# Sparse attention with a SoLU layer on one core: queries copied so that a block's columns lie together, the last tile in two banks, a new order

## The chip, the cores and the metric

The kernel runs on one core of a Trainium2 chip. The metric is the device time of one execution in microseconds; the time before is the median of three runs, 487.01 us (484.95 to 489.06). Smaller is better.

## What is computed

Attention over 8 batches, 8 heads, 576 positions and a head size of 64, in which four heads see the last 32 positions (local) and four see the positions with the same remainder modulo 32 (strided); then, for the 4608 tokens, a layer with two matrices, a softmax gate and a normalisation. Cut to what matters:

```python
scores = np.matmul(q, k.transpose(0, 1, 3, 2)) / np.sqrt(D)
mask_local = (rel >= 0) & (rel < 32)
mask_strided = (rel >= 0) & (pos[None, :] % 32 == pos[:, None] % 32)
attn = softmax(np.where(masks, scores, -1e9))     # heads 0-3 local, 4-7 strided
x = (attn @ v).transpose(0, 2, 1, 3).reshape(B * S, H * D)
...
h = x @ w_in                                      # 512 -> 1024
solu = h * softmax(h)
ln = (solu - mean(solu)) / sqrt(var(solu) + 1e-6) * g_ln
out = ln @ w_out                                  # 1024 -> 512
```

## The kernel before

All work is cut into steps, each a function that issues the instructions of one engine, with the tiles that it reads and writes. `Plan.add` (L128) records them in the order in which the program is written; a table of step numbers, `ORDER` (L61), found by a search, gives the order in which they are issued. Each engine works through its own steps in that order, and semaphores keep the dependencies.

Attention goes by units: each batch has two strided ones (6 and 5 blocks; a block is 3 remainders times 18 positions, 54 queries against 54 keys) and two local ones (5 and 4 blocks of 64 queries against 96 keys; in batch 0 they are 3 and 6). A unit (`unit`, L419) writes the mask into PSUM (L454, ACT; in batch 0 by PE, L463), adds the scores in float32 on PE (`qk`, L469), subtracts the row maximum, takes the exponential (L498), sums, scales on POOL (L507), splits the result into two float16 halves (L527, L529), transposes them by DMA (L534; batch 0 turns them on PE instead) and multiplies by the values (`pv`, L561). In batch 0 the units use L481 to subtract the maximum by a matmul, and the values stay in float32. Head pairs are placed so that four matmuls of 64 by 64 use the array side by side.

The queries lie in memory by position within the block, `q_raw` (L174), so one block's columns of a strided unit are 22 numbers apart and those of a local unit 18:

```python
q_raw[half][hs, q0 : q0 + (w - 1) * nqb + 1 : nqb]
```

The layer goes by 36 tiles of 128 tokens (`ff`). `g1` (L625 to L627) multiplies a tile by `w_in` in two halves of h, 512 columns each, 12 matmuls each (float16 high and low parts); DVE takes the maximum (L631), ACT the exponential (L635), DVE the product (L637), ACT the normalisation (L641, L642), POOL its small factors (L651 to L675), ACT and DVE the two float16 parts (L682, L683), a DMA transposes them (L686), and `g2` (L695 to L697) multiplies by `w_out`; ACT scales and stores a tile (L703, L704). Three banks of PSUM hold halves of h, one holds the out product.

Both matrices come as 64 bit numbers and are turned to float32 by `decode` (ACT L734, POOL L739, DVE L740), four blocks each; `prep_w` (L743) then forms `whi` (ACT, L761) and `wlo` (DVE, L762), and `prep_o` (L766) sums squares of `w_out` on PE (L777) and forms `ohi` (L786) and `olo` (L787). `v_scale` (L371) takes the size of a batch's values (L377), `v_split` (L396) their two float16 parts (L402, L403). `warm` (L246) issues matmuls whose results nobody reads.

The last tile's product is in one bank. ACT scales and stores its left half (L710, L711), DVE its right half (L714), which SP stores (L715).

Of the kernel before, what the change touches and what calls it, by code (L numbers as in the profile page):

```python
# [890 lines left out]
```

## Time and profile before

| | us |
|---|---|
| median of three runs | 487.01 |
| the three runs | 484.95, 489.06, 487.01 |
| the profiled execution | 488.86 |
| its span, from the first to the last instruction | 487.1 |

The rows that the prediction uses stand in a section below. In a row of the timeline the columns are start, duration, engine, line, operation, output and inputs, shapes and count, and in brackets the idle time of the engine before it with what ended it. PE is the engine of the matmuls, DVE, ACT and POOL the vector, scalar and general engines, SP the one that only issues DMAs; a q behind an engine's name is its queue of issues. One row can stand for several instructions of a kind (xcount), and then its duration is that of all of them.

### The profile page before, as it was taken

How to read it: one execution, taken by the hardware profiler on the slowest of the kernel's cores; microseconds unless marked ns; L12 is line 12 of the kernel's file. 1: busy time of each engine (PE TensorE's matmuls, PEld its weight loads, DVE VectorE, ACT ScalarE, POOL GpSimd, SP SyncE). 2: the span in 40 equal slices, each digit the busy share in tenths (PEclk: the TensorE clock that was granted, in tenths of full speed). 3: DMA queues.
4: the chain of work that ended last, by engine and by line, in shares of the span. 5: the costliest groups of instructions: out<-in, count | busy, mean ns of one | idle time of the engine just before them, and what ended most of it. 6: DMA issues, size and time to landing. Idle time of an engine off the chain costs nothing.

```text
span 487.1 us, 15063 instructions
## 1 busy us (share of the span) xinstructions
PE 470.0 (96%) x6436; PEld 244.0 (50%) x6436; DVE 326.5 (67%) x698; ACT 336.3 (69%) x555; POOL 168.5 (35%) x328
## 2 busy tenths in 40 slices
PE   8867989999999999999999999999999999999996
PEld 3645655555555555455454555545545544444442
DVE  0889799898788776777758666776656474444430
ACT  2498699798878878867675885855776565565450
POOL 5465425452623432242152314331234242232220
PEclk9995998999999999999999999999999999999999
DMA  8998689678979996657996992678573786405332
GB/s 331 419 372 321 182 189 261 141 163 228 183 186 201 209 222 125 175 78 166 268 163 138 250 220 72 109 155 157 128 132 62 137 148 115 87 23 129 74 84 81
DMA packets 131763, 83.87 MB, mean 172 GB/s; under 512 B 117424, under 2 KB 118288, under 8 KB 131184
## 3 DMA queue, kind: packets, MB, share of 16 engines
q1 hardware_dynamic: 126512, 73.60, 65.5%
q10 hardware_dynamic: 5184, 9.31, 5.6%
q8 instruction: 50, 0.82, 0.7%
q14 instruction: 17, 0.14, 0.1%
HBM read 39.90 MB, written 9.44 MB: 101 GB/s over the span
## 4 chain that ended last, share of the span: by engine, by line
PE 87%; DVE 5%; DMA 5%; issue 1%; SPq 0%; ACT 0%; ACTq 0%
PE o_ps L695 12%; PE h_ps L625 12%; PE h_ps L626 12%; PE o_ps L697 12%; PE h_ps L627 12%; PE o_ps L696 12%; PE s_ps L469 6%; PE x_ps L561 5%; DMA vrs<-vstr 3%; DMA q<-qstr 2%; DVE w L762 1%; DVE obuf L740 1%; DVE m L476 0%; DVE m L499 0%; DVE st L631 0%
## 5 line engine op out<-in xcount | busy, mean ns | idle before, releaser
L695 PE MATMUL o_ps<-ohi,cc 128*128 128x512 f16 x272 | 103.3, 380 | 0.0
L697 PE MATMUL o_ps<-ohi,cc 128*128 128x512 f16 x272 | 103.1, 379 | 0.0
L696 PE MATMUL o_ps<-obuf,cc 128*128 128x512 f16 x272 | 103.1, 379 | 0.0
L631 DVE TENSOR_REDUCE st<-h_ps 128x1 f32<-128x512 f32 x70 | 47.3, 684 | 42.6 <-PE h_ps L627 40.5
L507 POOL TENSOR_TENSOR t<-t,m 128x540 f32<-128x540 f32 (+5 forms) x32 | 42.7, 1339 | 87.9 <-DVE m L504 74.0
L683 DVE SCALAR_TENSOR_TENSOR cc<-raw,st,cc 128x1024 f16<-128x1024 f32 (+1 forms) x38 | 46.6, 1232 | 30.1 <-ACT cc L682 30.0
L635 ACT ACTIVATE raw<-h_ps,st,vsc 128x512 f32<-128x512 f32 x62 | 47.9, 775 | 23.5 <-DVE st L633 22.5
L626 PE MATMUL h_ps<-w,xl 128*128 128x512 f16 x140 | 54.0, 386 | 1.8 <-DVE obuf L740 1.8
L637 DVE SCALAR_TENSOR_TENSOR raw<-h_ps,raw 128x512 f32<-128x512 f32 x70 | 47.0, 682 | 12.2 <-ACT raw L635 11.4
L625 PE MATMUL h_ps<-w,xl 128*128 128x512 f16 x140 | 54.2, 387 | 0.3 <-DVE raw L637 0.3
L682 ACT ACTIVATE cc<-raw,st 128x1024 f16<-128x1024 f32 (+1 forms) x38 | 41.6, 1100 | 18.3 <-POOL st L672 17.3
L627 PE MATMUL h_ps<-w,xl 128*128 128x512 f16 x140 | 54.1, 386 | 0.0
L625 PE MATMUL h_ps<-w,xs 128*128 128x512 f16 x140 | 53.6, 383 | 0.0
L626 PE MATMUL h_ps<-w,xs 128*128 128x512 f16 x140 | 53.5, 382 | 0.0
L627 PE MATMUL h_ps<-w,xs 128*128 128x512 f16 x140 | 53.1, 379 | 0.0
L641 ACT ACTIVATE raw<-raw,st 128x1024 f32<-128x1024 f32 x36 | 41.2, 1144 | 16.7 <-DVE st L640 13.8
L697 PEld LDWEIGHTS <-cc 128*128 128x128 f16 x288 | 28.1, 98 | 34.0
L703 ACT ACTIVATE ob<-o_ps,st 128x512 f32<-128x512 f32 x34 | 23.2, 683 | 31.7 <-PE o_ps L697 25.9
L695 PEld LDWEIGHTS <-cc 128*128 128x128 f16 x288 | 28.1, 98 | 33.0
L696 PEld LDWEIGHTS <-cc 128*128 128x128 f16 x288 | 28.2, 98 | 32.1
L670 POOL TENSOR_SCALAR st<-st 128x1 f32<-128x1 f32 x32 | 8.8, 275 | 88.7 <-ACT raw L642 88.0
L642 ACT ACTIVATE raw<-raw 128x1024 f32<-128x1024 f32 x36 | 37.9, 1054 | 2.2 <-ACT ob L703 1.7
(187 smaller groups left out, 841.1 us busy)
## 6 DMA issues: line engine op xcount, KB each, us to landing
out<-ob ACTq DMA_DIRECT2D x35, 256.0 KB, 3.5
k<-kstr SPq DMA_DIRECT2D x8, 594.0 KB, 5.2
q<-qstr SPq DMA_DIRECT2D x8, 594.0 KB, 5.9
k<-kloc SPq DMA_DIRECT2D x8, 576.0 KB, 5.7
q<-qloc SPq DMA_DIRECT2D x8, 576.0 KB, 6.4
raw<-w_in SPq DMA_DIRECT2D x4, 1024.0 KB, 6.8
ve<-vl SPq DMA_DIRECT2D x7, 480.0 KB, 4.0
vrs<-vstr SPq DMA_DIRECT2D x4, 768.0 KB, 6.3
```

Source lines behind the costliest of these rows:

```text
L507: add("pool", nx * nk / 520 + 0.03, lambda: nc.gpsimd.tensor_tensor(t4, t4, sm2.unsqueeze(3).broadcast_to([P, 2, nb, nk]), op=ALU.mult), r ...
L625: nc.tensor.matmul(hv[i], xhi[cc], whi[:, cc, cols], start=(cc == 0), stop=False)
L626: nc.tensor.matmul(hv[i], xhi[cc], wlo[:, cc, cols], start=False, stop=False)
L627: nc.tensor.matmul(hv[i], xlo[cc], whi[:, cc, cols], start=False, stop=(cc == 3))
L631: add("dve", 0.69, lambda i=i: nc.vector.tensor_reduce((nm, nm2)[i], hv[i], axis=AX.X, op=ALU.max, negate=True), r=[HH[i]], w=[(ST, "nm", i)])
L635: add("act", 0.73, lambda i=i, q=q: nc.scalar.activation(e[:, parts2[i]], hv[i], AF.Exp, bias=nm, scale=hs, accum_out=q), r=[HH[i], (ST, " ...
L637: add("dve", 0.7, lambda i=i, x=x: nc.vector.scalar_tensor_tensor(u[:, parts2[i]], hv[i], 1.0, e[:, parts2[i]], op0=ALU.mult, op1=ALU.mult ...
L682: add("act", w / 1200 + 0.295, lambda cols=cols: nc.scalar.mul(c[:, 0, cols], u[:, cols], r), r=[(U, 0), (U, 1), (ST, "r")], w=CC[0][mine])
L683: add("dve", w / 980 + 0.23, lambda cols=cols: nc.vector.scalar_tensor_tensor(c[:, 1, cols], u[:, cols], r, c[:, 0, cols], op0=ALU.mult, o ...
L695: nc.tensor.matmul(o, ct[:, cc, :], ohi[:, cc, :], start=(cc == 0), stop=False)
L696: nc.tensor.matmul(o, ct[:, cc, :], olo[:, cc, :], start=False, stop=False)
L697: nc.tensor.matmul(o, ct[:, 8 + cc, :], ohi[:, cc, :], start=False, stop=(cc == 7))
```

## The change

Queries first. From batch 2 on the strided queries are copied in float32, and in batches 6 and 7 the local ones too, so that the columns of a block are contiguous; the copies are on ACT for the strided ones of odd batches, on POOL otherwise. They lie in memory that was free at that time (`qc` behind the second set of raw values, `ql` in the unused half of `obuf`). The last tile's out product is cut at column 384 into two banks, and DVE writes its part into another buffer. Twelve more warm matmuls (`LATE`) can stand before `prep_o`. The order is searched anew for all steps. `V_PE` is empty, so the branch that it guards isn't taken; two cost entries of the plan change, which set no instruction by themselves.

```diff
+END = 384
+LATE = 6
+BLOCKED = (2, 3, 4, 5, 6, 7)
+BLOCKED_LOC = (6, 7)
 ORDER = """
-0-1 27 2 30 24 22 50 3-10 51 56 52 31 28 23 35 11 32-34 25 43 20 12 26 13 57 38 14-15 102 44 37 103-104 58 86 53 21
+1 3-5 39 31 28 6-9 22 2 34-35 20 44 32 27 23 33 10 46 29 56 11 79 30 86 102 45 87 103 25 88 104-105 38 12 58 57 13 106
...
+    ql = obuf[:, :, 256:512].rearrange("p c (x i) -> p c x i", i=QL)
+    qc = [more[:, VW[0] + VW[1] + i : VW[0] + VW[1] + j] for i, j in ((0, 12 * QS), (12 * QS, 2 * SP))]
+    NB2 = SP // QS
...
+    def by_block(b):
+        for j, (_, b0, nb) in enumerate(LATER[0:2]):
+            w = 2 * nb * QS
+            dst = qc[j][:, 0:w].rearrange("p (c x i) -> p c x i", c=2, x=nb)
+            src = q_raw[1][:, 0 : 2 * SP].rearrange("p (i c x) -> p c x i", c=2, x=NB2)[:, :, b0 : b0 + nb]
+            r, wr = [("q", 1)], [("qc", j), *([("roomq",)] if b == BLOCKED[0] else [])]
+            if b % 2:
+                add("act", w / 1200 + 0.3, lambda dst=dst, src=src: nc.scalar.copy(dst, src), r=r, w=wr)
+            else:
+                add("pool", w / 480 + 0.1, lambda dst=dst, src=src: nc.gpsimd.tensor_copy(dst, src), r=r, w=wr)
+
+    def local_by_block(b):
+        src = q_raw[0][:, 0 : 2 * S].rearrange("p (i x) -> p x i", x=2 * NBL)
...
+            nc.gpsimd.tensor_copy(ql[:, 0:4], src[:, 0:16].rearrange("p (c x) i -> p c x i", x=4))
+            nc.gpsimd.tensor_copy(ql[:, 4, 0 : 2 * NBL - 16], src[:, 16 : 2 * NBL])
...
+                        if blocked and not half:
+                            x = pair * NBL + b0 + i
+                            q = ql[hs, x // 4, x % 4, a : a + w]
+                        elif blocked:
+                            q = qc[j][hs, (pair * nb + i) * QS : (pair * nb + i + 1) * QS]
...
-        add("pe", nb * (0.212, 0.2)[half] + ((0.27, 0.14) if by_pe else (0.008, 0.195))[half], qk,
+        add("pe", nb * 0.145 + 0.195 if blocked and half else nb * (0.212, 0.2)[half] + ((0.27, 0.14) if by_pe else (0.008, 0.195))[half], qk,
...
+            sides = [(o[:, 0:END], O, slice(0, END)), (s_ps[:, 0, END:DM], ("s", 0), slice(END, DM))]
...
-            add("dve", 0.42, lambda: nc.vector.tensor_scalar(ob[:, ends[1]], o[:, ends[1]], f, None, op0=ALU.mult), r=[O, (ST, "f"), OB], w=[(*OB, 1)])
+            ob2, OB2 = e_sb[(n + 1) % 2], [(("e", (n + 1) % 2), y) for y in range(2)]
+            add("dve", 0.3, lambda: nc.vector.tensor_scalar(ob2[:, rc], right, f, None, op0=ALU.mult), r=[RIGHT, (ST, "f")], w=OB2)
...
+            for i in range(LATE):
+                add("pe", 0.4, lambda: warm(2, [h_ps[1][:, 0:480]]), r=["ones"], w=[("h", 1)])
```

Three places in the order. The first is SP's queue at the start of the program, before, where `w_in` and `w_out` are the matrices, `kstr` and `qstr` the strided keys and queries, `vloc` the local values:

```order
L346 DMA raw_67<-w_in 128x2048 x2
L268 DMA mask_80<-masks 128x288
L346 DMA k_66<-kstr 128x1188
L346 DMA q_64<-qstr 128x1188
L796 DMA g_119<-g 128x8
```

and now:

```order
L355 DMA vl_70<-vloc 128x1280
L277 DMA mask_80<-masks 128x288
L355 DMA q_64<-qstr 128x1188
L355 DMA k_66<-kstr 128x1188
L355 DMA raw_67<-w_in 128x2048 x2
```

Two blocks of `w_in` went from ahead of the strided queries and keys to behind them, and the local values came to the front.

The second is ACT in the start-up, around the last quarter of `whi` (the row that writes `w_114`); `obuf` is where `w_out` is turned to float32, `s_ps<-mask` the mask of the next unit. Before:

```order
L761 ACTIVATE w_114<-cc_104,w_sc_116 128x1024
L454 COPY s_ps<-mask_80 128x2x270
L522 ACTIVATE pt_99<-o_ps,vsc_76 128x384
L582 CAST xl_100<-x_ps 128x2x64
L582 CAST xl_100<-x_ps 128x2x2x64
L498 ACTIVATE t_85<-t_85 128x648
L734 ACTIVATE obuf_115<-raw_67 128x1024 x2
L402 ACTIVATE vs_72<-vrs_69,vsc_77 128x1536
L522 ACTIVATE pt_99<-h_ps,vsc_76 128x384
L734 ACTIVATE obuf_115<-cc_104 128x1024
L498 ACTIVATE t_86<-t_86 128x540
L454 CAST s_ps<-mk_loc_81 128x2x320
```

and now:

```order
L793 ACTIVATE obuf_115<-raw_67 128x1024
L793 ACTIVATE obuf_115<-cc_104 128x1024
L550 ACTIVATE t_85<-t_85 128x648
L634 CAST xl_100<-x_ps 128x2x64
L574 ACTIVATE pt_99<-h_ps,vsc_76 128x384
L550 ACTIVATE t_86<-t_86 128x540
L634 CAST xl_100<-x_ps 128x2x2x64
L499 CAST s_ps<-mk_loc_81 128x2x320
L820 ACTIVATE w_114<-cc_104,w_sc_116 128x1024
L579 CAST p_94<-t_85 128x12x54
L446 ACTIVATE vl_70<-vrl_68,vsc_77 128x1280
L400 ACTIVATE vs_71,vm_74<-raw_67 128x1536
```

What stood behind the last quarter stands ahead of it now.

The third is where the copies stand. On ACT, ahead of batch 5's first strided unit (its mask is the row `s_ps<-mask_80 128x2x324`; `raw_67,st` are the exponentials of an h tile), it reads before:

```order
L635 ACTIVATE raw_67,st_108<-h_ps,st_108 128x512
L682 ACTIVATE cc_104<-raw_67,st_107 128x1024
L641 ACTIVATE raw_67<-raw_67,st_108 128x1024
L454 COPY s_ps<-mask_80 128x2x324
L635 ACTIVATE raw_67,st_109<-h_ps,st_109,vsc_79 128x512 x2
```

and now:

```order
L446 ACTIVATE vl_70<-raw_67,vsc_76 128x1280
L550 ACTIVATE t_88<-t_88 128x512
L421 COPY raw_67<-q_64 128x648
L421 COPY raw_67<-q_64 128x540
L579 CAST p_96<-t_87 128x2x320
L499 COPY s_ps<-mask_80 128x2x324
L687 ACTIVATE raw_67,st_109<-h_ps,st_109,vsc_79 128x512 x2
```

The two copies stand three places ahead of the exponentials. On POOL, batch 2's copies now stand here, among the multiplies and subtractions of batch 1 (before, the same rows without them):

```order
L559 TENSOR_TENSOR t_86<-t_86,m_89 128x540
L581 TENSOR_TENSOR p_94<-t_85,p_94 128x12x54
L423 COPY raw_67<-q_64 128x648
L581 TENSOR_TENSOR p_95<-t_86,p_95 128x2x5x54
L423 COPY raw_67<-q_64 128x540
L704 TENSOR_SCALAR st_107<-st_107 128x1
```

The small steps of the first tile's norm follow them.

## Rows read from the trace of the kernel before

**Rows 1.** The page: the span, then busy us, share and instructions by engine.

```profile
span 487.1 us, 15063 instructions
...
PE 470.0 (96%) x6436; PEld 244.0 (50%) x6436; DVE 326.5 (67%) x698; ACT 336.3 (69%) x555; POOL 168.5 (35%) x328
```

**Rows 2.** Stages: length, busy us (x instructions) by engine, clock, DMA share, GB/s.

```profile
core 0: us, PE busy (x) PEld busy (x) DVE busy (x) ACT busy (x) POOL busy (x), PEclk, DMA share, GB/s
72.00:76.00 4.00, 3.88 (x17) 1.61 (x18) 4.00 (x8) 3.97 (x8) 0.00 (x0) 0.57 0.84 117
200.00:220.00 20.00, 20.00 (x134) 9.49 (x132) 14.41 (x31) 13.41 (x22) 6.15 (x14) 1.00 0.65 127
460.00:480.00 20.00, 20.00 (x94) 9.05 (x93) 5.91 (x12) 8.29 (x14) 2.62 (x8) 1.00 0.38 93
```

**Rows 3.** PE in order of time: half of an h, later a strided scores unit.

```profile
144.17 0.38 PE L625 MATMUL h_ps<-w,xl 128*128 128x512 f16 x1
...
146.76 0.38 PE L625 MATMUL h_ps<-w,xl 128*128 128x512 f16 x1
...
150.39 1.46 PE L469 MATMUL s_ps<-k,q 64*54 64x54 f32 x48
151.79 0.39 PE L625 MATMUL h_ps<-w,xl 128*128 128x512 f16 x1
```

**Rows 4.** PE in order of time, in the first 46 us.

```profile
11.55 1.26 PE L469 MATMUL h_ps<-k,q 64*54 64x54 f32 x40 [1.14 <-DMA q<-qstr]
...
15.52 0.63 PE L753 MATMUL x_ps<-cc 128*128 128x128 bf16 x8 [0.27 <-DVE cc L740]
...
19.71 1.27 PE L469 MATMUL h_ps<-k,q 64*32 64x64 f32 x96
...
30.54 0.92 PE L561 MATMUL x_ps<-pt,vs 54*64 54x54 f32 x48 [0.76 <-ACT pt L522]
...
45.77 0.59 PE L626 MATMUL h_ps<-w,xl 128*128 128x512 f16 x1 [1.84 <-DVE obuf L740]
```

**Rows 5.** Groups of one line by form: busy us, mean ns of one.

```profile
L481 PE MATMUL h_ps<-m,minus 128*128 128x384 f32 x4 | 1.5, 485 | 0.0
...
L481 PE MATMUL s_ps<-m,minus 128*128 128x192 f32 x4 | 0.9, 338 | 0.0
```

**Rows 6.** Groups of ACT and of POOL: operations of a unit's size.

```profile
L454 ACT COPY s_ps<-mask 128x648 f32<-128x648 f32 x7 | 4.9, 701 | 0.1
...
L507 POOL TENSOR_TENSOR t<-t,m 128x648 f32<-128x648 f32 x8 | 12.0, 1501 | 4.9 <-DVE m L504 4.9
```

**Rows 7.** DMA issues of one kind: count, KB each, median us to landing.

```profile
q<-qstr SPq DMA_DIRECT2D x8, 594.0 KB, 5.9
```

**Rows 8.** The end in order of time: last matmul, ACT, DVE, the right store.

```profile
482.85 0.38 PE L697 MATMUL h_ps<-ohi,cc 128*128 128x512 f16 x1
...
483.32 0.47 ACT L710 ACTIVATE ob<-h_ps,st 128x256 f32<-128x256 f32 x1 [4.54 <-PE h_ps L697]
...
483.83 0.48 DVE L714 TENSOR_SCALAR ob<-h_ps,st 128x256 f32<-128x256 f32 x1 [11.00 <-ACT ob L710]
484.34 0.36 SPq L715 DMA_DIRECT2D out<-ob  x1
```

**Rows 9.** A stage early on, columns as in rows 2.

```profile
8.00:12.00 4.00, 2.86 (x32) 1.43 (x33) 0.00 (x0) 1.12 (x1) 3.28 (x10) 1.00 1.03 417
```

**Rows 10.** ACT in order of time, around the weights' last quarter.

```profile
38.06 1.19 ACT L761 ACTIVATE w<-cc,w_sc 128x1024 f16<-128x1024 f32 x1
...
48.89 0.69 ACT L454 CAST s_ps<-mk_loc 128x640 f32<-128x640 bf16 x1
53.35 0.78 ACT L635 ACTIVATE raw<-h_ps,st,vsc 128x512 f32<-128x512 f32 x1 [3.77 <-DVE st L633]
```

**Rows 11.** The chain of waits: start us, us, what.

```profile
46.35 0.43 PE h_ps L627
...
81.87 0.32 PE o_ps L695
```

More of the change, by code (lines that the diff above doesn't have):

```diff
@@ L253, in attn_solu_kernel @@
         add("pe", 0.4, lambda: warm(2, [o_ps[:, 0:480]]), r=["ones"], w=["o"])
-    add("dve", 0.1, lambda: nc.vector.memset(s_ps[:, 1, 504:512], 0.0), w=[("s", 1)])
+    add("dve", 0.1, lambda: nc.vector.memset(s_ps[:, 1, 480:512], 0.0), w=[("s", 1)])
     def mask_strided():
@@ L389, in v_scale, with fn @@
         add("dve", 0.41, hscale, r=[("vsc", b % 4), "w_sc"], w=[("hsc", b % 4)])
+    def by_block(b):
[6 more added lines that the diff above has]
+                add("act", w / 1200 + 0.3, lambda dst=dst, src=src: nc.scalar.copy(dst, src), r=r, w=wr)
+            else:
+                add("pool", w / 480 + 0.1, lambda dst=dst, src=src: nc.gpsimd.tensor_copy(dst, src), r=r, w=wr)
+    def local_by_block(b):
+        src = q_raw[0][:, 0 : 2 * S].rearrange("p (i x) -> p x i", x=2 * NBL)
+        first = [("od", c) for c in range(8)] if b == BLOCKED_LOC[0] else []
+        def fn():
+            nc.gpsimd.tensor_copy(ql[:, 0:4], src[:, 0:16].rearrange("p (c x) i -> p c x i", x=4))
+            nc.gpsimd.tensor_copy(ql[:, 4, 0 : 2 * NBL - 16], src[:, 16 : 2 * NBL])
+        add("pool", 2 * S / 480 + 0.2, fn, r=[("q", 0)], w=["ql", *first])
     def o_factor(b):
@@ L452, in unit @@
         by_pe = b == 0
+        blocked = b in (BLOCKED_LOC, BLOCKED)[half]
         if not by_pe:
@@ L691, in ff, with g2 @@
                     r=CC[k][mine], w=[(*CT, y, k)], issue=(0.5, 2.5))
-        def g2(i):
+        sides = [(o, O, slice(0, DM))]
+        if n == NT - 1:
+            sides = [(o[:, 0:END], O, slice(0, END)), (s_ps[:, 0, END:DM], ("s", 0), slice(END, DM))]
+        def g2(i, dst, cols):
             for cc in range(4 * i, 4 * i + 4):
-                nc.tensor.matmul(o, ct[:, cc, :], ohi[:, cc, :], start=(cc == 0), stop=False)
-                nc.tensor.matmul(o, ct[:, cc, :], olo[:, cc, :], start=False, stop=False)
-                nc.tensor.matmul(o, ct[:, 8 + cc, :], ohi[:, cc, :], start=False, stop=(cc == 7))
+                nc.tensor.matmul(dst, ct[:, cc, :], ohi[:, cc, cols], start=(cc == 0), stop=False)
+                nc.tensor.matmul(dst, ct[:, cc, :], olo[:, cc, cols], start=False, stop=False)
+                nc.tensor.matmul(dst, ct[:, 8 + cc, :], ohi[:, cc, cols], start=False, stop=(cc == 7))
         for i in range(2):
-            add("pe", 2.62, lambda i=i: g2(i), r=[(*CT, i, 0), (*CT, i, 1), *(("o_w", cc) for cc in range(4 * i, 4 * i + 4))], w=[O])
+            for dst, D_, cols in sides:
+                add("pe", 2.62 * (cols.stop - cols.start) / DM, lambda i=i, dst=dst, cols=cols: g2(i, dst, cols),
+                    r=[(*CT, i, 0), (*CT, i, 1), *(("o_w", cc) for cc in range(4 * i, 4 * i + 4))], w=[D_])
         def store():
```

163 lines of the change are left out of this document (91 added, 72 removed).

## Prediction

> **What bounds the kernel now.** I read the page first: over a span of 487.1 us PE is busy for 470.0, while ACT and DVE stand at 69% and 67% and POOL at 35% [rows 1]. A busy PE need not run at its peak, so the stages come next: from 200 to 220 us and from 460 to 480 us PE is busy for 20.00 of 20 us at full clock, and no other engine comes near that (ACT 13.41, DVE 14.41 in the former) [rows 2]. Then I look at PE in order of time: twelve matmuls of one half of h start between 144.17 and 146.76, one every 0.216 us, without a hole, and a strided scores unit stands directly between other matmuls: it starts at 150.39 and the next h matmul at 151.79 [rows 3]. So after the start-up time taken off PE's work comes off the end, as long as the other engines keep up. The start-up differs: at 72 to 76 us DVE and ACT are busy for 4.00 and 3.97 of 4 us and PE's clock is 0.57 [rows 2], ACT and DVE are the limit there, and the first out-matmul of a token tile is at 81.87 [rows 11]. The end is a third place: behind the last matmul stand two evacuations in a row and a store [rows 8].
>
> **Strided scores.** A strided unit of six blocks is 24 matmuls, 48 records in the trace (a float32 matmul leaves two), and takes 1.46 us [rows 3]; less the last record's 0.27 (the mean length of this form, 1.46 - 47 x 25.3 ns) a record starts every 25.3 ns. Six batches have 11 blocks with 8 records each: 528 records at this pace are 13.4 us. What pace would contiguous columns have? The nearest row is the product with values in batch 0: float32 too, 54 columns stream through, and its stationary operand is contiguous; 48 records take 0.92 us, so with 0.22 for the last a record starts every 14.9 ns [rows 4]. That would save 528 x 10.4 ns = 5.5 us. Bounds: nothing, if the stride isn't what slows it; and the streaming pass: 384 columns take 485 ns and 192 take 338, 0.77 ns per column and record [rows 5], so 54 columns, four records at a time, can't go below 10.4 ns, which would save 7.9 us. The plan's own cost for a block goes from 0.2 to 0.145 us in the diff, 3.6 us for 66 blocks; its old entry fits the trace (6 x 0.2 + 0.195 = 1.40, the distance of the two starts in rows 3). I take 5.0, nearer to the row.
>
> **Local scores of batches 6 and 7.** 96 records take 1.27 us [rows 4], with 0.23 for the last 10.9 ns each. Here 32 columns are loaded and 64 stream. At the contiguous pace of 14.9 ns for 54 columns, 32 would need 8.8 ns; if streaming with eight at a time sets the pace, 64 x 0.77 / 8 = 6.2 ns. Two batches have 288 records: 0.6 us by the first, 1.4 by the second, 0 if the stride costs nothing here. I take 0.5. [...]
>
> **The copies.** Each of the six batches copies 648 and 540 columns, on POOL for even batches and on ACT for odd ones; two local copies of 1152 columns are on POOL. ACT's copy of 648 columns takes 0.70 us [rows 6], so odd batches add about 1.3 us each, 4 in all to a busy time of 336. POOL's multiply of 648 columns takes 1.50 us [rows 6]; a copy has one operand less, so I put 0.7 to 1.5, and all POOL copies come to at most 13 us on an engine that is busy for 168 of 487. I cost them at nothing: PE's other matmuls cover them. The cover is gone if scores are due before their copy: the scores no longer wait for the query transfer (5.9 us to landing [rows 7]) but for the transfer and then a copy in a queue of POOL or ACT. In batch 2 POOL copies between two subtractions of batch 1; behind it stand the tile's norm steps. A wait there would hold those, then ACT's scaling. PE waited for no query transfer but the first, 1.14 us [rows 4], so transfers have been early; some 2 us more of lead is wanted.
>
> **The end.** The last matmul ends at 482.85 + 0.38 = 483.23. ACT starts 0.09 later and takes 0.47; DVE starts only at 483.83, right behind ACT, takes 0.48, and its store is issued at 484.34; the span ends 2.76 us later [rows 1, 8]. With two banks DVE need not wait for ACT: it starts 0.09 behind the last matmul with half the columns (between 0.24 and 0.48 us, I take 0.36), and its store goes out 0.48 behind the last matmul where it was 1.11: 0.63 saved. ACT's part of 384 columns ends one run of twelve narrow matmuls earlier, so its 0.55 us (0.47 and the slope to rows 6) are covered. PE pays for splitting: 24 matmuls of 384 and 24 of 128 columns; the narrow one costs between a quarter of 0.216 and 0.63 / 8 = 0.079 [rows 4], so 0 to 0.6 us, mostly the former, 0.1. Together -0.5 (0 to -0.9).
>
> **The start-up.** Two changes of order have opposite signs. First, transfers: between 8 and 12 us they run at 417 GB/s with all engines busy [rows 9], and the first strided scores wait until 11.55 for q [rows 4]. Two blocks of w_in, 1024 KB each, stood ahead of it; now 640 KB of v do. 1408 KB less at this rate is 3.4 us earlier for the first scores and what hangs on them. Second, ACT converts the last quarter of w at 38.06; the 10.3 us of ACT work from its end to 49.58 (masks, turned weights, three more blocks of w_out, batch 1's first v, exponentials) [rows 10] now stand ahead of it. h needs all quarters, so its steady row, from 45.77 [rows 4], comes up to 10.3 - 3.4 = 6.9 us later. That isn't all lost: ACT waited 3.77 us for tile 0 [rows 10] and now has the second v, squares and w_out's scaling to do, and PE had slack: between 45.77 and 81.87 lie 36.1 us, of which eight halves of h are 8 x 2.59 = 20.7, and four scores units, four value products and three squares of w_out about 10.3 (an estimate at the paces of rows 3 and 4). The other 5 us are waits and matmuls at 0.43 instead of 0.22 us at the slow clock [rows 11]. So this term lies between 5 us gained (PE's slack all used) and 6.9 - 5 = 1.9 lost; I take 1.5 gained. The added warm matmuls stand ahead of the last three squares of w_out, before the wait for w, so I count no clock for them (0 to 1.6: rows 11's pace was slow for some 3.2 us at 46).
>
> **The sum.** 5.0 + 0.5 + 0.5 + 1.5 = 7.5 us. The profiled execution took 488.86, which would give 481.4; it lies 1.85 above the median of the three runs, 487.01, and the runs spread from 484.95 to 489.06. Taken off the median: 479.5.
>
> **Rivals.** (a) The start-up eats part: the later w holds PE back, 1.9 us lost. For it: ACT and DVE are full there [rows 2] and PE starts h with a cold clock whatever comes before. Against it: ACT's idle 3.77. Time: 487.0 - 6.0 + 1.9 = 482.9. (b) The pace isn't the stride's: a record keeps 25.3 ns because of the switching between heads and blocks, and the copies are vain. For it: no row shows these 54 columns contiguous. Against it: 14.9 ns in a product with the same switching [rows 4]. Time: 487.0 - 0.5 - 1.5 = 485.0. (c) Slower: ACT's copies in batches 3, 5 and 7 are read too early in its queue and wait for q's transfer, 5.9 us [rows 7]; behind them stand the exponentials that free the banks of h, so PE runs dry. Three times 5.9 is 17.7: 487.0 - 7.5 + 17.7 = 497. It decides from 12.4 us of PE waits, 4.1 per odd batch. For it: in batch 5 the two copies stand directly ahead of the mask and of a tile's exponentials. Against it: ACT is idle for over 6 of 20 us in the middle [rows 2], and PE has out-matmuls to go on with. (d) More than forecast: the full 5.5, the local share and most of PE's slack: 487.0 - 11 = 476.
>
> **How the numbers follow.** About 1% (4.9 us) is what a measurement of this kernel can tell from no change. Forecast (477.5 to 482.1) 0.52, (a) 0.20, (b) 0.10, (c) 0.06, (d) 0.12. Under 482.1 lie the forecast, (d) and some of (a): 0.70 faster; the rest of (a) and (b), 0.24, within 1%; (c) slower, 0.06. The range reaches from 474.5 (most of the upper bounds) to 486.5 (all of (b)); (c) and the extremes stay out.
>
> **What would show it.** In the changed profile the strided unit's 48 records should take 0.9 to 1.1 us instead of 1.46 with less time per weight load; ACT's copies about 0.7 and 0.6 us without a wait for q; no PE wait at scores behind a copy after 100 us; DVE's last step within 0.15 us of the last matmul; the first out-matmul near 80 us. The prediction is wrong if scores keep 25 ns per record, if the first out-matmul is later than 84, or if ACT's copies wait for transfers by more than 4 us each.

## The result, and the profile after

The changed kernel takes 492.28 us (median of 8 runs, 490.52 to 495.43), the kernel before in the same comparison 487.24 (8 runs, 484.46 to 489.06). The ratio is 1.0111, 95% interval 1.0077 to 1.0146: slower by 1.1%, where a faster kernel, 479.5, was forecast, with a range of 474.5 to 486.5. The profiled execution is the longest of the eight, 495.43 us, and the one with the lowest granted clock (0.972, median 0.986); where a size matters I use ratios or several profiles.

The page of the changed kernel, span and busy times (before: [rows 1]):

```profile
span 493.7 us, 15166 instructions
PE 473.1 (96%) x6472; PEld 243.7 (49%) x6472; DVE 329.2 (67%) x698; ACT 343.6 (70%) x561; POOL 183.4 (37%) x338
```

PE is busy 3.1 us longer than before, not less, and 20.6 us of the span are idle against 17.1. Yet the copied scores are quicker. PE in order of time, the strided unit of six blocks that answers to 150.39 in [rows 3], and the groups of PE's scores by form:

```profile
217.43 0.82 PE L520 MATMUL s_ps<-k,raw 64*54 64x54 f32 x48 [0.74 <-ACT s_ps L499]
...
L520 PE MATMUL s_ps<-k,raw 64*54 64x54 f32 x528 | 9.3, 213 | 0.8 <-ACT s_ps L499 0.7
```

48 records in 0.82 us: (0.82 - 0.213) / 47 = 12.9 ns each, where it was 25.3. 528 times 12.4 is 6.5 us taken off, more than the 5.0 forecast. The end works too (the timeline at the end, before: [rows 8]):

```profile
490.35 0.22 PE L753 MATMUL s_ps<-ohi,cc 128*128 128x128 f16 x1
...
490.71 0.35 DVE L773 TENSOR_SCALAR raw<-s_ps,st 128x128 f32<-128x128 f32 x1 [10.54 <-PE s_ps L753]
491.09 0.36 SPq L774 DMA_DIRECT2D out<-raw  x1
```

DVE starts 0.14 us behind the last matmul and the span ends 3.13 behind it (3.87 before). So 7 us were taken off PE's work and 5 us were added to the time: some 12 must have been lost elsewhere. PE in order of time around its first h matmul, in the kernel before (the next one stands at 45.77 in [rows 4]):

```profile
43.30 0.63 PE L625 MATMUL h_ps<-w,xl 128*128 128x512 f16 x1
```

and from 40 us on in the changed kernel:

```profile
41.08 1.19 PE L613 MATMUL x_ps<-pt,vs 54*64 54x54 f32 x40 [1.54 <-DVE xs L635]
...
48.62 0.43 PE L613 MATMUL x_ps<-pt,ve 64*64 64x32 f32 x4 [1.32 <-DMA ve<-vloc]
...
50.26 0.98 PE L257 MATMUL h_ps<-ones 128*128 128x480 bf16 x2
51.03 1.91 PE L836 MATMUL o_ps<-obuf 128*128 128x128 bf16 x16
...
55.74 1.42 PE L520 MATMUL s_ps<-k,q 64*32 64x64 f32 x80
57.10 0.61 PE L677 MATMUL h_ps<-w,xl 128*128 128x512 f16 x1
...
85.76 0.51 PE L751 MATMUL o_ps<-ohi,cc 128*128 128x512 f16 x1 [0.38 <-DMA cc<-cc]
```

The first h matmul comes 13.8 us later, and the unbroken row of them 11.3 later (from 57.10, where it was 45.77). Ahead of it PE waits, issues a pair of warm matmuls and two squares of w_out, then value products and a scores unit; from 48.62 on it works without a hole. The first out-matmul is at 85.76 instead of 81.80 (the chain of [rows 11] counts the same matmul from 81.87).

A half of h also needs all quarters of w, and w is late too (timelines of ACT and DVE around 50 us, of SP at 29 to 39):

```profile
50.18 0.27 ACT L634 CAST xl<-x_ps 128x128 f16<-128x128 f32 x1 [2.53 <-PE x_ps L613]
...
52.24 1.17 ACT L820 ACTIVATE w<-cc,w_sc 128x1024 f16<-128x1024 f32 x1
...
53.83 1.28 DVE L821 SCALAR_TENSOR_TENSOR w<-cc,w_sc,w 128x1024 f16<-128x1024 f32 x1
```

```profile
29.25 7.28 SPq L355 DMA_DIRECT2D raw<-w_out  x2
37.38 0.37 SPq L355 DMA_DIRECT2D cc<-w_out  x1
37.80 1.39 SPq L355 DMA_DIRECT2D ve<-vloc  x3
```

Here is a chain through four queues: SP issues the loads of ve (a second arrangement of batch 0's local values) only at 37.80, behind two loads of w_out that hold its queue for 7.28 us; PE's value product waits for ve; ACT's cast waits 2.53 us for that product; and the last quarter of whi stands behind the cast and starts at 52.24 instead of 38.06 [rows 10]. With wlo on DVE, w is complete at 55.11, where it was 41.85. But that is 2.0 us before the first h matmul: PE came to h late by its own order, not by a wait for w.

The earlier quarters of w were late as well, although the new order of the transfers was to bring things forward. In the kernel before, the last square of w_in (w's scale comes from these squares), the first quarter of whi and the last steps of wlo:

```profile
25.61 0.62 PE L753 MATMUL x_ps<-cc 128*128 128x128 bf16 x8
31.44 1.16 ACT L761 ACTIVATE w<-cc,w_sc 128x1024 f16<-128x1024 f32 x1
39.39 2.46 DVE L762 SCALAR_TENSOR_TENSOR w<-cc,w_sc,w 128x1024 f16<-128x1024 f32 x2
```

and in the changed kernel the first scores, the last square of w_in and the first quarter of whi:

```profile
9.76 1.46 PE L520 MATMUL s_ps<-k,q 64*54 64x54 f32 x48 [1.11 <-DMA k<-kstr]
29.28 0.64 PE L812 MATMUL x_ps<-cc 128*128 128x128 bf16 x8 [1.14 <-DVE cc L799]
34.05 1.15 ACT L820 ACTIVATE w<-cc,w_sc 128x1024 f16<-128x1024 f32 x1
```

The first scores start 1.8 us earlier (11.55 in [rows 4]). But the blocks of w_in, which now all come behind the strided queries and keys, are turned to float32 later (ACT waits for the last one's transfer until 25.48, before until 22.57), so the last square is 3.7 us later and the first quarter of whi 2.6.

Meanwhile the clock (4 us windows of PE; columns: window, length, PE busy and instructions, granted clock, DMA share, GB/s):

```profile
36.00:40.00 4.00, 2.83 (x57) 1.00 0.71 234
40.00:44.00 4.00, 2.92 (x79) 0.69 0.98 323
44.00:48.00 4.00, 3.19 (x38) 0.50 1.00 227
48.00:52.00 4.00, 3.38 (x56) 0.50 1.02 413
52.00:56.00 4.00, 4.00 (x129) 0.50 1.01 409
56.00:60.00 4.00, 4.00 (x91) 0.68 0.16 61
```

Ahead of the fall PE was idle for 1.2 of 4 us and waited for DVE at 41.08. From 44 to 56 us the granted clock was 0.50, and it came back to 1.00 only after the h matmuls had begun (0.50 from 56 to 58 us, 0.85 from 58 to 60, 1.00 from 60 to 62). The kernel before has such a stretch too, at 0.50 from 40 to 48 us and at 0.92 from 48 to 52.

### The profile page after: what moved, and what is told of

It is laid out like the page before. It is cut to its first block, busy times and chain, and to the rows that moved or that the text cites. A ratio compares the mean times of both kernels' runs of the same rounds, so it can differ in the third digit from the quotient of the medians.

```text
span 493.7 us, 15166 instructions
## 1 busy us (share of the span) xinstructions
PE 473.1 (96%) x6472; PEld 243.7 (49%) x6472; DVE 329.2 (67%) x698; ACT 343.6 (70%) x561; POOL 183.4 (37%) x338
## 4 chain that ended last, share of the span: by engine, by line
PE 74%; DMA 8%; DVE 7%; ACT 6%; issue 3%; SPq 2%; POOL 1%; ACTq 0%; DVEq 0%; POOLq 0%
PE o_ps L751 11%; PE o_ps L752 11%; PE o_ps L753 11%; PE h_ps L677 10%; PE h_ps L679 9%; PE h_ps L678 9%; PE x_ps L613 5%; PE s_ps L520 4%; DMA raw<-w_in 3%; DMA ve<-vloc 2%; DMA cc<-cc 1%; SPq L355 1%; DMA ve<-vl 1%; DVE st L683 1%; ACT raw L687 1%
## 5 line engine op out<-in xcount | busy, mean ns | idle before, releaser
L752 PE MATMUL o_ps<-obuf,cc 128*128 128x512 f16 x272 | 104.4, 384 | 2.6 <-issue 2.6
L751 PE MATMUL o_ps<-ohi,cc 128*128 128x512 f16 x272 | 104.6, 384 | 0.4 <-DMA cc<-cc 0.4
L753 PE MATMUL o_ps<-ohi,cc 128*128 128x512 f16 x272 | 104.5, 384 | 0.0
L559 POOL TENSOR_TENSOR t<-t,m 128x648 f32<-128x648 f32 (+5 forms) x32 | 40.8, 1280 | 49.4 <-DVE m L556 45.2
L722 POOL TENSOR_SCALAR st<-st 128x1 f32<-128x1 f32 x32 | 7.7, 242 | 131.7 <-ACT raw L694 131.3
L677 PE MATMUL h_ps<-w,xl 128*128 128x512 f16 x140 | 53.5, 382 | 0.8 <-DVE raw L689 0.8
L679 PE MATMUL h_ps<-w,xl 128*128 128x512 f16 x140 | 53.3, 381 | 0.0
L678 PE MATMUL h_ps<-w,xl 128*128 128x512 f16 x140 | 53.3, 381 | 0.0
L753 PEld LDWEIGHTS <-cc 128*128 128x128 f16 x296 | 29.2, 99 | 35.4 <-issue 2.7
L752 PEld LDWEIGHTS <-cc 128*128 128x128 f16 x296 | 29.2, 99 | 34.6 <-issue 3.6
L751 PEld LDWEIGHTS <-cc 128*128 128x128 f16 x296 | 29.2, 99 | 33.8 <-issue 1.4
## 6 DMA issues: line engine op xcount, KB each, us to landing
raw<-w_in SPq DMA_DIRECT2D x4, 1024.0 KB, 13.8
```

Of the source, the lines that this page charges most:

```text
L677: nc.tensor.matmul(hv[i], xhi[cc], whi[:, cc, cols], start=(cc == 0), stop=False)
L678: nc.tensor.matmul(hv[i], xhi[cc], wlo[:, cc, cols], start=False, stop=False)
L679: nc.tensor.matmul(hv[i], xlo[cc], whi[:, cc, cols], start=False, stop=(cc == 3))
L751: nc.tensor.matmul(dst, ct[:, cc, :], ohi[:, cc, cols], start=(cc == 0), stop=False)
L752: nc.tensor.matmul(dst, ct[:, cc, :], olo[:, cc, cols], start=False, stop=False)
L753: nc.tensor.matmul(dst, ct[:, 8 + cc, :], ohi[:, cc, cols], start=False, stop=(cc == 7))
```

## The experiments

Sixteen kernels. "Old" is the order of the kernel before with the copies put in some 30 steps ahead of their scores, "new" that of the changed kernel, both as lists of the same steps. They ran on different chips (the kernel before: 485.9 to 487.2 us there), so I compare ratios to the kernel before on the same chip, and "scaled" is that ratio times 487.0.

| kernel | us, median | ratio (95%) | scaled |
|---|---|---|---|
| changed kernel | 492.28 | 1.0111 (1.0077 to 1.0146) | 492.4 |
| e1 old order, copies | 482.74 | 0.9925 (0.9896 to 0.9953) | 483.3 |
| e2 new order, no copies | 495.48 | 1.0169 (1.0114 to 1.0224) | 495.2 |
| e3 changed kernel, ve early | 490.61 | 1.0109 (1.0040 to 1.0177) | 492.3 |
| e4 layout by the host, old order | 479.25 | 0.9847 (0.9803 to 0.9891) | 479.5 |
| e5 old start-up, new rest | 487.47 | 1.0003 (0.9981 to 1.0026) | 487.1 |
| e6 new start-up, old rest | 493.33 | 1.0133 (1.0103 to 1.0162) | 493.5 |
| e7 layout by the host, old order, two banks | 479.26 | 0.9839 (0.9807 to 0.9872) | 479.2 |
| e8 layout by the host, new order | 488.34 | 1.0038 (1.0011 to 1.0065) | 488.9 |
| e9 only SP's start-up new | 501.12 | 1.0319 (1.0266 to 1.0371) | 502.5 |
| e10 all start-up new but SP's | 507.77 | 1.0443 (1.0396 to 1.0490) | 508.6 |
| e11 changed kernel, no added warm | 488.71 | 1.0054 (1.0024 to 1.0084) | 489.6 |
| e12 old order, copies on POOL | 480.64 | 0.9893 (0.9855 to 0.9930) | 481.8 |
| e14 old order, copies on ACT | 483.57 | 0.9964 (0.9942 to 0.9987) | 485.2 |
| e15 e11 with ve early | 487.27 | 1.0038 (1.0007 to 1.0070) | 488.9 |
| e16 e6 without added warm | 489.76 | 1.0086 (1.0057 to 1.0115) | 491.2 |
| e18 e15 with w early | 495.27 | 1.0217 (1.0176 to 1.0258) | 497.6 |

**Is it the order or the copies?** Theory: the new order loses the time. Rival: the copies do. One kernel has the copies without the order, one the order without the copies, and one moves a single suspect, the loads of ve.

```diff
-LATE = 6
+LATE = 0
-ORDER = new
+ORDER = old
```

> All parts of the change (copies, two banks at the end) in the order of before: every step that both kernels have stands in the order of before, and each copy is put some 30 steps ahead of its scores; no added warm matmuls. The changed kernel's strided unit of six blocks takes 0.82 us where it took 1.46, so 528 records save about 6.5 us, and the end saves about 0.6. Theory O (the new order costs the time, in the start-up and at a stall around 140 us): 479 to 482 us. Rival C (the copies, 1.4 us each on ACT and 1.4 to 2.6 on POOL, hold up the engines behind them): 486 to 490 us. If both hold in part: between.

```diff
-BLOCKED = (2, 3, 4, 5, 6, 7)
-BLOCKED_LOC = (6, 7)
+BLOCKED = ()
+BLOCKED_LOC = ()
```

> The new order without the copies: the scores read the strided queries as before, the copy steps are left out, all else as in the changed kernel. Theory O: the 6.5 us of PE's saving are lost and nothing comes back, 496 to 500 us. Rival C: the stalls go with the copies, 486 to 490 us. A middle value of 491 to 494 would say that the copies gave back about what they saved.

```diff
-SP: raw<-w_out x2, cc<-w_out, ve<-vloc x3
+SP: ve<-vloc x3, raw<-w_out x2, cc<-w_out
```

> The changed kernel with one move: the three loads of the second arrangement of batch 0's local values stand ahead of the second block of w_out in SP's queue, as they nearly did before, and not behind the fourth. Theory V (these loads, held up in the queue until 37.8 us, hold PE at the local products of batch 0 and with them the first h matmul): the first h matmul 2 to 5 us earlier than 57.1 and the time 488 to 490.5. Rival (PE's own order is what makes h late: two squares of w_out, the second local product and a scores unit stand ahead of it): no more than 1.5 us earlier, 491 to 493.

Measured: 482.74, 495.48 and 490.61. Copies in the old order are faster than the kernel before by 0.75%; the new order without copies is slower by 1.7%. The rival falls: with the copies, the new order and its added warm matmuls (the old order has none) lose about 9 us (492.4 against 483.3 scaled). Moving ve alone brought nothing clear of its interval; the first h matmul came at 55.49, 1.6 us earlier.

**The stride alone.** The host lays the queries contiguously, for all batches; the kernel reads them as they lie, without a copy; order and end as before.

```diff
-q_raw[half][hs, q0 : q0 + (w - 1) * nqb + 1 : nqb]
+q_raw[half][hs, q0 : q0 + w]
-"qstr": by_query(lay_qk(q, False, SP), QS),
+"qstr": lay_qk(q, False, SP),
...
```

> The kernel of before, in its order, with queries that the host lays out so that the columns of a block lie together when they are loaded; no copies, one bank at the end, all batches and both kinds of units. If the contiguous pace alone is what the change brings and PE bounds the time after 80 us: 7 batches save 616 x 12.4 ns = 7.6 us, a little more for local units, so 478.5 to 481. Rival G (the time saved on PE is given back to another engine's limit): 483 to 487.

Measured: 479.25, within the forecast. PE's groups by form, first of the kernel before, then of this one:

```profile
L469 PE MATMUL s_ps<-k,q 64*54 64x54 f32 x664 | 21.2, 269 | 2.6 <-issue 1.6 <-ACT s_ps L454 1.0
L469 PE MATMUL s_ps<-k,q 64*32 64x64 f32 x1056 | 15.3, 235 | 0.0
```

```profile
L469 PE MATMUL s_ps<-k,q 64*32 64x64 f32 x1056 | 14.1, 224 | 0.3 <-DMA q<-qloc 0.3
L469 PE MATMUL s_ps<-k,q 64*54 64x54 f32 x664 | 12.7, 218 | 2.8 <-issue 1.7 <-ACT s_ps L454 1.0
```

The strided scores fall from 21.2 to 12.7 us and the local ones from 15.3 to 14.1, with nothing else changed; 7.5 of these 9.7 us reach the end (scaled 479.5).

**Where in the order?** The two orders are joined at the first out-matmul, either way round. Two more kernels have the host's layout and two banks, one in each order, without copies and without added warm matmuls.

```diff
-LATE = 6
+LATE = 0
-ORDER = new
+ORDER = old[:319] + [s for s in new if s not in old[:319]]
```

> The first 319 steps (all that is issued up to the first out-matmul, no added warm matmuls) stand in the order of the kernel before with batch 2's copies put in; all later steps stand in the new order. With the old order throughout and the copies the time was 482.7, with the new one throughout 492.3, so 9.6 us are to be shared out. Theory S (the new start-up costs them): 483 to 486, and the first out-matmul at 81 to 83 us. Theory M (the order behind the start-up costs them): 489 to 492 with the same early out-matmul. A share of half each gives 486 to 489.

```diff
-ORDER = new
+ORDER = new[:337] + [s for s in old if s not in new[:337]]
```

> The counterpart: the first 337 steps in the new order, with the six added warm steps, all later steps in the old order with the copies. Theory S: 489 to 492, with the first out-matmul at 84 to 87 us. Theory M: 483 to 486. Half each: 486 to 489. If both this kernel and the one with the old start-up come out above 489, two orders joined fit badly and the pair says nothing on the share.

```diff
-ORDER = new
+ORDER = old
-q = q_raw[half][hs, q0 : q0 + (w - 1) * nqb + 1 : nqb]
+q = q_raw[half][hs, q0 : q0 + w]
```

> Old order, queries laid contiguously by the host (no copies), last tile in two banks. The same with one bank took 479.25. If the two banks bring what the trace of the end shows (0.6 us less from the last matmul to the end): 478.3 to 479.0. If the end is worth nothing: 479.0 to 479.8. Fastest of all kernels so far by either.

```diff
-q = q_raw[half][hs, q0 : q0 + (w - 1) * nqb + 1 : nqb]
+q = q_raw[half][hs, q0 : q0 + w]
```

> New order without the added warm matmuls, queries laid contiguously by the host, no copies, two banks. If the order costs the same whatever the queries' layout (theory O): 487 to 489.5, some 9 above the old order with the same layout. If the order's cost comes from copies that stand in its way or from the strided pace that it wasn't searched for (theory C): 479 to 483.

Measured: 487.47, 493.33, 479.26 and 488.34. With the host's layout, too, the new order costs 9.7 us (scaled, no added warm matmuls in either), so its loss doesn't hang on the copies. The new start-up before the old rest is as slow as the whole change, beyond what theory S said. The old start-up before the new rest lies in the band of half each; it loses 3.8 against old throughout, but its trace shows a wait that only the joint makes (PE's waits):

```profile
PE o_ps L750 <- DVE obuf L844: 2.7, 1, 2.7
```

The first out-matmul waits 2.7 us for a part of w_out that DVE now forms too late; neither parent has that wait. Less that wait, this pair gives the start-up most of the loss and the rest about 1 us. The two banks can't be told from one bank by time (479.2 and 479.5, intervals overlap).

**Which part of the start-up?** SP's queue can be exchanged by itself in the old order, and so can the other four engines. Neither of these two kernels has added warm matmuls. Then the added warm matmuls are taken out of the changed kernel, and out of the joined one.

```diff
-ORDER = old
+ORDER = SP: new start-up, then old; PE, ACT, DVE, POOL: old
```

> Old order with copies (482.7) in which SP's queue alone begins in the new order (32 of its 153 places differ: two blocks of w_in behind the strided queries and keys, the values of batch 0 first, ve<-vloc behind w_out); PE, ACT, DVE and POOL keep the old order. With the new start-up on all five engines, and the old order behind it, it was 493.3: 10.6 us are to be shared out. Theory T (the order of transfers costs them): 488 to 493, first h matmul at 50 us or later. Theory P (the order on the computing engines costs them): 481 to 485, first h matmul at 43 to 46 us.

```diff
-ORDER = old
+ORDER = PE, ACT, DVE, POOL: new start-up, then old; SP: old
```

> The counterpart: PE, ACT, DVE and POOL begin in the new order (61, 79, 121 and 28 places differ), SP's queue keeps the old one, all old behind the start-up; no added warm matmuls. Theory T: 482 to 486. Theory P: 490 to 494, the first h matmul still later than 52 us. If both this one and the one with SP's queue alone changed are slow, the orders of SP and of the other engines need each other, and neither alone is the cause.

```diff
-LATE = 6
+LATE = 0
```

> The changed kernel without its twelve added warm matmuls, all else in the new order, copies kept (changed kernel: 492.3). The trace has these twelve at 3.6 us of PE's busy time in the kernel with the new start-up. If they stand in PE's way: 488 to 489.5. If they only fill a wait: 491.5 to 493. If they keep the clock up, as warm matmuls are meant to: 493 to 496.

The same edit on the kernel with the new start-up and the old rest:

> New order up to the first out-matmul without the added warm matmuls, old order behind it, copies (with the warm matmuls: 493.3; old order throughout: 482.7). If the added warm matmuls cost 3.6 us here too: 489 to 490.5, and the start-up's order by itself costs 6.5 to 8, as much as the whole new order without them (6.0). If the start-up without them is harmless and the rest costs the 6.0: 483 to 485.

Measured: 501.12, 507.77, 488.71 and 489.76. Both halves of the exchange are far slower than either whole order, so theories T and P both fall, and what was expected if both are slow holds: the two parts need each other. In the first, PE waits 12.8 us for a mask and 4.9 for ve (PE's waits):

```profile
PE h_ps L506 <- POOL ob L264: 12.8, 1, 12.8
PE x_ps L611 <- DMA ve<-vloc: 4.9, 1, 4.9
```

The added warm matmuls cost 2.8 us scaled in the changed kernel and 2.3 with the old rest. In the changed kernel they take 4.7 us of PE (its groups by form):

```profile
L257 PE MATMUL h_ps<-ones 128*128 128x480 bf16 x12 | 4.7, 512 | 0.0
```

Without them the new start-up still costs 7.9 us scaled (491.2 against 483.3), and the new order behind it nothing (489.6 against 491.2). That the 4.7 us are what the warm matmuls cost isn't shown: with the old rest, the profile with them has its first out-matmul earlier than the one without (82.77 against 85.07) and loses its time behind that.

**The mechanism within it.** ve early, and then also the last quarter of w early on ACT and DVE, with tile 0's h ahead of a value product.

```diff
-LATE = 6
+LATE = 0
-SP: raw<-w_out x2, cc<-w_out, ve<-vloc x3
+SP: ve<-vloc x3, raw<-w_out x2, cc<-w_out
```

> Changed kernel without the added warm matmuls (488.7) and with the three loads ve<-vloc ahead of the last blocks of w_out in SP's queue. In that kernel PE waits 2.1 us for ve at 46 to 48 us and the clock is at half behind it, 0.64 from 40 to 60 us. If that wait and the clock behind it carry a part of the 6.0 us that the new order still costs: 486 to 487.5, and a granted clock over 0.70 from 40 to 60. If not: 488 to 489.5.

```diff
-ACT: xl<-x_ps, xl<-x_ps, w<-cc
+ACT: w<-cc, xl<-x_ps, xl<-x_ps
-DVE: obuf<-obuf,raw, obuf<-obuf,cc, w<-cc
+DVE: w<-cc, obuf<-obuf,raw, obuf<-obuf,cc
-PE: x_ps<-pt,vl, s_ps<-k,q, h_ps<-w x24
+PE: h_ps<-w x24, x_ps<-pt,vl, s_ps<-k,q
```

> As the kernel without warm matmuls and with early ve, and besides: the last quarter of whi on ACT ahead of the tile's casts (in the changed kernel it starts at 52.2 us, in the one before at 38.1), wlo behind it on DVE, and tile 0's two halves of h on PE ahead of the value product and the scores of units 3 and 6. If the late quarter is what the start-up loses: 483 to 485.5, first h matmul at 49 to 52 us. If PE's order makes no difference because the same work is only exchanged: within 1 us of the kernel with early ve.

Measured: 487.27, and 495.27. The first is a small gain (489.6 to 488.9 scaled, intervals overlap), with the clock at 0.81 from 40 to 60 us where it was 0.64. The second is a miss of both its answers. w's quarter started at 48.17, but wlo now stood ahead of the DVE steps that turn the last blocks of w_out to float32, and the squares of w_out, which PE still had ahead of h, waited for those (PE in order of time):

```profile
52.96 1.89 PE L834 MATMUL o_ps<-obuf 128*128 128x128 bf16 x16 [4.67 <-DVE obuf L797]
54.64 0.63 PE L675 MATMUL h_ps<-w,xl 128*128 128x512 f16 x1
```

So an early w by itself doesn't repair the start-up: the first h matmul came at 54.64, 0.65 us later than in the kernel with ve early, with w complete for 4.0 us. The same four moments in seven traces (us; w is complete when wlo's last step on DVE ends):

| kernel | last quarter of whi starts | w complete | first h matmul | first out-matmul |
|---|---|---|---|---|
| before | 38.06 | 41.85 | 43.30 | 81.80 |
| e1 old order, copies | 38.13 | 41.92 | 43.66 | 78.00 |
| changed kernel | 52.24 | 55.11 | 57.10 | 85.76 |
| e11 no added warm | 51.62 | 54.10 | 56.13 | 83.97 |
| e16 new start-up, old rest | 51.71 | 54.19 | 56.71 | 85.07 |
| e15 ve early | 50.78 | 53.26 | 53.99 | 83.13 |
| e18 ve and w early | 48.17 | 50.62 | 54.64 | 89.78 |

In none of the last five does PE wait at its first h matmul; w is complete 0.7 to 4.0 us ahead of it. So w's lateness and PE's own order end close together there, and curing one meets the other. Nor is ve what makes w late: with ve early, ACT's wait for the product is 0.27 us instead of 3.08, but it waits 1.51 us for a block of w_out instead, and the quarter starts only 0.8 us sooner (50.78 against 51.62). Between e16 and e1, which have the same order behind the start-up, the delay is 13.1 us at the first h matmul, 7.1 at the first out-matmul and 8.5 at the end of the profile.

**What the clock has to do with it.** Windows of 20 us, PE alone, of the old order with copies:

```profile
20.00:40.00 20.00, 13.95 (x304) 0.96 1.02 365
40.00:60.00 20.00, 19.88 (x351) 0.87 0.85 279
```

and of the changed kernel without added warm matmuls:

```profile
20.00:40.00 20.00, 14.04 (x240) 0.77 0.93 364
40.00:60.00 20.00, 16.95 (x350) 0.64 0.79 270
```

In windows of 1 us the traces of the kernel before and of the changed kernel show 1.00 or 0.50, and other values only next to a change from one to the other (5 of 487 and 8 of 493 windows). With these two levels a mean of c over 20 us is 40 (1 - c) us at the lower one: 1.6 + 5.2 = 6.8 in the first, 9.2 + 14.4 = 23.6 in the second. The pages give PE busy for 461.3 and 468.9 us with the same matmuls: 7.6 us more for 16.8 at the lower clock, about 0.4 us for each. That is busy time, in one profile of either order. Time itself shows less. Over 168 executions of the 18 kernels, each against the mean of its kernel on its chip, 0.24 us of time go with each us at the lower clock (95% 0.20 to 0.28; us at the lower clock are 2 (1 - c) times the span). By their median granted clocks the executions spend 10.6 us there in the old order with copies, 24.3 in the changed kernel without added warm matmuls and 22.0 with the new start-up and the old rest; but 13.7 in the changed kernel itself, no more than in the kernel before (11.6 to 15.5 by chip), and 10.3 with the new start-up, the old rest and the added warm matmuls. By this estimate the clock carries some 3 us of the 6.3 and 7.9 that the two kernels without added warm matmuls lose against the old order, and less than 1 of the 9.1 of the changed kernel. No run held the clock fixed.

**Do the copies give anything back?** All on POOL, then all on ACT, in the old order.

```diff
-            if b % 2:
+            if False:
```

> Old order with copies (482.7) and with all strided copies on POOL, none on ACT. Layout by the host without copies, two banks, old order: 479.3, so the copies give back 3.5 us. If ACT's three batches of copies give it back (PE waited 3.7 us for masks that ACT writes into the scores' bank): 479.5 to 481.5. If POOL's copies do (PE waited 3.0 us for DVE's product, and a copy on POOL and an operation of DVE were seen to hold each other): 483 to 485.5.

```diff
-            if b % 2:
+            if True:
```

> Old order with copies, all six batches' strided copies on ACT (three on ACT: 482.7, none on ACT: 480.6). If ACT's copies cost 2.1 us for three batches because masks and exponentials stand behind them: 484.3 to 486. If the difference of those two kernels was not the engine's: 482 to 483.3.

Measured: 480.64, as the first theory said, and 483.57, between its two answers; with three batches on ACT it was 482.74. Scaled: none on ACT 481.8, three 483.3, six 485.2: 0.5 to 0.6 us per batch. Each step lies inside the intervals, the whole of it does not. The changed kernel's copies of 648 columns on ACT and on POOL (groups by form):

```profile
L421 ACT COPY raw<-q 128x648 f32<-128x648 f32 x3 | 4.9, 1625 | 0.0
```

```profile
L423 POOL COPY raw<-q 128x648 f32<-128x648 f32 x3 | 5.8, 1947 | 0.0
```

ACT's copy of 648 columns takes 1.63 us, not the 0.70 of [rows 6], which is a copy of as many contiguous columns into PSUM. In the old order with copies one stands ahead of casts and a mask for the next scores, and PE waits for that mask (ACT, then PE, in order of time):

```profile
209.49 1.38 ACT L419 COPY raw<-q 128x540 f32<-128x540 f32 x1
...
217.16 0.60 ACT L497 COPY s_ps<-mask 128x540 f32<-128x540 f32 x1
...
217.81 0.72 PE L518 MATMUL s_ps<-k,raw 64*54 64x54 f32 x40 [1.58 <-ACT s_ps L497]
```

Such waits sum to 3.7 us over five units there, to 1.9 over three with all strided copies on POOL, but to 2.8 over four with all of them on ACT, the slowest of the three. So they alone don't explain the cost.

## Why the prediction was wrong

**Strided scores: right, and under-sized.** 6.5 us by the trace against 5.0 (bounds 0 and 7.9). The nearest row, 14.9 ns, was taken nearly whole; the record came to 12.9. Rival (b), that the pace isn't the stride's, falls: the copied scores and the host's layout both show it. The copies read the same columns, 88 bytes apart: 1.63 us on ACT against 0.70 for as many contiguous ones, though into another memory, so how much of it is the stride's isn't shown. I priced the copy by the contiguous row.

**Local scores: right in size.** 80 records took 1.14 us and now 1.04 in the changed kernel, some 0.4 us for the 288, where 0.5 was said; the host's layout gives 1.2 for 1056.

**Copies at nothing: wrong, by about 1.5 us.** That is what the three batches on ACT cost (481.8 against 483.3 scaled), in a row with the six (485.2). One way is seen, through ACT's queue to the masks that the scores wait for; that it is the only one isn't shown, as those waits don't grow with the copies. Rival (c) named that queue, but another mechanism: ACT's copies never waited for a transfer, their idle time is 0.0.

**The end: right in the trace** (0.74 us less behind the last matmul), too small for the runs to show.

**Start-up: the step that failed.** It was "between 5 us gained and 1.9 lost; I take 1.5 gained". Exchanged by itself, the start-up's order loses 7.9 us (e16 against e1). The working was that h comes up to 10.3 - 3.4 = 6.9 us later and that PE's slack of 5 us pays for most of it. The delay is the term that was mis-sized: in the changed kernel the row of h matmuls is 11.3 us later and the last quarter of whi 14.2.

First, the 3.4 us of head start. I took the move of two blocks of w_in as a gain for the queries and didn't follow what hangs on these blocks, the squares and w's scale. The third quarter of whi starts 1.7 us later (37.40 against 35.72) instead of 3.4 earlier, 5.1 of the 7.3 us (14.2 - 6.9) by which the quarter missed. Second, the 10.3 us that moved ahead of the last quarter. They were read as work, but ACT is idle for 1.9 of them; in the changed kernel this stretch adds 12.5, of which ACT is idle for 3.6, mostly for a product of PE. I followed the step past its own engine's work, but not past that engine's waits. Third, I let w alone set the time of h. In the changed kernel PE's own order set it, with value products, squares and scores ahead of h, 2.0 us behind the end of w. The slack was about right: 13.1 us at the first h matmul became 7.1 at the first out-matmul, so 6 were paid where 5 were said.

The added warm matmuls are a term that the sum put at nothing: it allowed them 0 to 1.6 us of clock and counted none of PE's time. They cost 2.8, with the higher clock (median 0.986 with them, 0.975 without) already in it.

Rival (a) had the place and the sign, and gave 1.9; its mechanism, that w holds PE back, isn't what the traces show. The slow clock at the start of h was there in each of eight traces, in the old order and the new: the first h matmul took 0.61 to 0.63 us, later on one took 0.38. How the 7.9 us divide among late w_in, ACT's waits, PE's order and the clock stays open: ve early gains 0.7 us with overlapping intervals, and w early on top of it loses 8.7. The prediction named a first out-matmul later than 84 us as a sign that it was wrong; it was at 85.76.

**The sum, redone** (scaled): 487.0, copies and end in the old order -3.7, the new start-up +7.9, the order behind it -1.6 (not clear of nothing), the added warm matmuls +2.8: 492.4. One gap stays open: scores, end and the copies' price come to -6.5 - 0.4 - 0.7 + 1.5 = -6.1, but the old order with copies brought -3.7 (-5.1 to -2.3).

The fastest are the two kernels with the host's layout and the old order, 479.2 and 479.5 scaled, ahead of both kernels; with the layout of the inputs left as it is, it is the old order with all strided copies on POOL, 481.8.

## What to carry to other kernels

With its columns 88 bytes apart the stationary operand cost as much again here as the matmul with contiguous ones (25.3 ns per record against 12.9): compare the pace of a record with that of a contiguous product of the same size, and lay the operand out where it is made. When an order is replaced as a whole, price its start-up apart: follow each moved step through every wait in front of it to the queue that ends last, and through what hangs on each transfer that moves back. Then look whether the engine that bounds the time really waited there, or was busy with its own order. Two orders can each be better whole than with one queue exchanged (483.3 and 491.2 against 502.5 and 508.6 here), so test a part by exchanging a closed stretch, and look for waits that only the joint makes.

## What was not expected of the hardware

A copy on POOL and an operation of DVE, side by side, both took longer than others of their forms. In the changed kernel (DVE and POOL in order of time):

```profile
50.00 0.17 DVE L555 TENSOR_SCALAR m<-m 128x12 f32<-128x12 f32 x1
...
136.12 1.27 DVE L735 SCALAR_TENSOR_TENSOR cc<-raw,st,cc 128x1024 f16<-128x1024 f32 x1
136.26 2.61 POOL L423 COPY raw<-q 128x648 f32<-128x648 f32 x1
137.32 1.59 DVE L555 TENSOR_SCALAR m<-m 128x12 f32<-128x12 f32 x1
```

The copy began while DVE's product ran and took 2.61 us; the other two of its form took 1.61 and 1.62. The small operation behind the product took 1.59 us, where the median of its nine is 0.17, and ended with the copy (138.91 and 138.87). That the one stretched the other is my reading.

With the added warm matmuls the clock was higher, and the kernel was slower all the same. Over all executions the median granted clock was 0.986 with them and 0.975 without in the changed kernel, 0.990 and 0.978 with the new start-up and the old rest: some 11 us less at the lower clock each time, for 2.8 and 2.3 us more. One profile can mislead here: that of the changed kernel shows 0.57 from 40 to 60 us with them and 0.64 without.
